# Shifts of transposed heads by pairs, and the reads of the second half's hash bits ahead of the normalized rows' transposing transfer

## The chip, the cores and the metric

The kernel runs on one core of one Trainium2 chip. The time is the device time of one execution in microseconds (us); of the kernel before, three runs are shown. Engines: PE is TensorE (matrix products), DVE VectorE, ACT ScalarE, POOL GpSimd, and SP is SyncE, which here only issues transfers (DMAs). Each engine works through its own queue in order; SP's queue too: an issue that waits for something holds up all issues behind it.

## The reference, cut to what matters

Attention in which a query sees only the keys of the same hash bucket (six signs of a projection make the bucket), and behind it a normalization and a two-layer perceptron with a residual, over 4 batches of 8 heads, 768 rows and 64 elements per head.

```python
q_bits = (einsum('bhsd,dk->bhsk', q, proj) > 0)        # 6 bits; k_bits likewise
mask = q_bucket[:, :, :, None] == k_bucket[:, :, None, :]
scores = where(mask, q @ k.T / sqrt(D), -1e9)
attn = softmax(scores) @ v                             # x: heads side by side, 512 wide
xn = (x - mean(x)) / sqrt(var(x) + 1e-6) * g_ln
out = x + relu(xn @ w_ch1) @ w_ch2                     # 512 -> 2048 -> 512
```

## The kernel before, in words

The rows of a batch are worked on in chunks of 256 query rows, three to a batch, twelve in all. Stage n runs the attention of chunk n on TensorE and ScalarE: twelve units, three to a pair of heads, each with scores (L530), exponentials (L540), products with the values (L565) and, at a pair's end, the division (L585 to L592). The scores of the next unit are emitted ahead of the products of the present one. Heads come in pairs 0 and 1, 2 and 3, 4 and 5, 6 and 7; the first two pairs are the first half, the others the second.

The mask is made by the scores' product itself. The operand tile `slots` (two of them, batches taking turns) holds for each head 64 rows of transposed data and under them, in rows 64 to 69, the six bits as plus or minus a large number: a product over 70 rows then gives the score plus a term that sinks all keys of other buckets.

For batches 1 to 3 these operands are prepared during earlier stages, a half (four heads) at a time, by steps with one letter each, followed by the batch and the half (J11: batch 1, second half):

- L loads queries and keys, W the values (SP; for batch 1 GpSimd's queue).
- N (`narrow`, L357) casts them to bf16 on GpSimd.
- T (`operands`, L380) issues four transposing transfers on SP, one per head. The queries and keys of a head become six blocks of 128 columns in 128 rows: rows 0 to 63 hold one chunk of rows of the sequence, rows 64 to 127 the next one.
- P (`shifted`, L388) is one transfer on SP that copies rows 64 to 127 of the four heads to rows 0 to 63 of the other six blocks of the same heads: 384 KB.
- B (`blocks`, L362) transposes 32 by 32 blocks on VectorE, H (`hashes`, L397 to L414) multiplies them with the projection on TensorE, turns the products into bits on VectorE and writes them to a tile in DRAM, `bits_d`, by SP.
- J (`bit_rows`, L420) issues four transfers on SP, one per head, that read `bits_d` into rows 64 to 69 of all twelve blocks of the head, 18 KB each. As P reads rows 64 to 127 of six of these blocks, J's transfer for a head has to come behind P's for this head.
- V (and Y, Z) casts and sums the values on GpSimd; Q sums squares on ScalarE.

The order within a stage is written out by hand in a dictionary of strings, `steps` (L927 on). Beside the letters above, `n` stands for the normalization of the chunk before (`norm`, L630 on): statistics and centring on VectorE, then on SP one transposing transfer of the normalized rows, `xnT<-xn` (L641), which waits for VectorE. `u` is one of eight up-projections (L674) with its rectification, the first of which needs `xnT`; `d` is one of eight parts of a down-projection (L715), after each fourth of which SP issues an output store (L724). The function `interleave` spreads this list evenly over the units, so that the engines' queues hold the steps in the order of the string. SP gets T, P, J, H's write, L, W, n's transfer and d's stores in that order.

In stage 2 the second half of batch 1 is prepared up to its shift (T11, H11, P11), and its reads of bits, J11, are the second word of stage 3, behind `n`. The scores that first need them are those of heads 4 and 5 in stage 3.

Of the kernel before, what the change touches and what calls it, by code (L numbers as in the profile page):

```python
# [30 lines left out]
def kernel(  # L31
# [11 lines left out]
    nc = tc.nc  # L43
    P = 128

    B, H, S, D = q.shape
# [146 lines left out]
    class Prep:  # L193
# [191 lines left out]
        def shifted(self, half):  # L385

            dst = self.pair_places(half)
            nc.sync.dma_start(out=dst[0:D, :, 1], in_=dst[D:P, :, 0])  # L388

        def hashes(self, half):  # L390

# [455 lines left out]
    def first_two():  # L847
# [77 lines left out]


    steps = {  # L927
# [284 lines left out]
```

## Time and profile before

| What | us |
|---|---|
| Median of 3 runs | 307.48 |
| Lowest and highest run | 304.97 and 308.14 |
| The profiled execution | 306.8 |
| Its span, first to last instruction | 305.0 |
| TensorE busy in it | 294.8 |
| ScalarE busy | 216.8 |
| VectorE busy | 179.8 |
| GpSimd busy | 91.0 |

The lines of the profile that follow give for an instruction its start in us from the span's start, its duration in us, its engine (SPq is SP's queue, PEld TensorE's weight load), its line in the kernel, its operation and `out<-in` by the names of the tiles; `x4` counts instructions that were merged into one line, and brackets hold the idle time of the engine before it and what ended it. A transfer's line on SPq covers its issue, not its landing. In the chain of work (lines without a line's tile sizes) a piece marked DMA runs from the issue to the landing. In the lists of waits stand the waiting operation, what it waited for, us in total, the number of times, and the longest. The lines of a source line's instructions give the shortest, the median and the longest duration in ns and the first and last start in us.

### The profile page before, as it was taken

Reading aid. Unit: us, or ns where it says so; the run is one execution under the profiler, and the core shown is the slowest. Engines: PE = TensorE matmul, PEld = TensorE weight load, DVE = VectorE, ACT = ScalarE, POOL = GpSimd, SP = SyncE. Lnnn points to the kernel's source line nnn. Section 1 sums busy time; section 2 is a strip of 40 time slices with the busy share of each in tenths; the row PEclk is TensorE's granted clock in tenths of the full one; section 3 lists DMA queues with packets and bytes.
Section 4 is the critical chain, followed back from the end, with each engine's and each line's share of the span. In section 5 each row is a group of like instructions: output and inputs, shape, how many; then the busy total and the mean of one; then the engine's idle time right before and its main releaser. Section 6 shows DMA issues by size and latency. Waiting matters only on the chain.

```text
span 305.0 us, 7962 instructions
## 1 busy us (share of the span) xinstructions
PE 294.8 (97%) x3279; PEld 224.6 (74%) x3306; DVE 179.8 (59%) x420; ACT 216.8 (71%) x271; POOL 91.0 (30%) x119
## 2 busy tenths in 40 slices
PE   8899999999899999999999999999999999999994
PEld 6577896687587688678688678679678678687573
DVE  2778568755287576645865874834734745645422
ACT  3898987767687787788698688778698568575020
POOL 2999721791011145160650740100100100100200
PEclk9999999999999999999999999999999999999998
DMA  7999999949589767695397365330220200200302
GB/s 214 359 220 252 250 242 242 191 82 151 98 261 204 155 212 128 176 289 138 97 234 192 109 111 124 41 89 2 21 84 2 69 37 2 71 35 2 105 2 74
DMA packets 58617, 40.93 MB, mean 134 GB/s; under 512 B 38576, under 2 KB 53424, under 8 KB 58576
## 3 DMA queue, kind: packets, MB, share of 16 engines
q1 hardware_dynamic: 53712, 30.80, 44.4%
q0 software_dynamic: 4288, 8.91, 12.5%
q10 hardware_dynamic: 576, 0.66, 0.7%
q8 instruction: 27, 0.44, 0.6%
q14 instruction: 14, 0.11, 0.1%
HBM read 27.98 MB, written 6.88 MB: 114 GB/s over the span
## 4 chain that ended last, share of the span: by engine, by line
PE 76%; DMA 7%; POOL 5%; ACT 4%; DVE 3%; issue 2%; SPq 2%; POOLq 0%; ACTq 0%; DVEq 0%
PE hp L674 25%; PE o L715 19%; PE sc L530 17%; PE av L565 9%; ACT ex L540 3%; DMA qnat<-in_q_dram 2%; PE hash L397 2%; DMA slots<-slots 1%; SPq L380 1%; POOL vsum L440 1%; PE o L697 1%; DMA xnT<-xn 1%; PE tpose L231 1%; POOL vaug L431 1%; POOL nat L357 1%
## 5 line engine op out<-in xcount | busy, mean ns | idle before, releaser
L540 ACT ACTIVATE ex<-sc,expb 128x1024 bf16<-128x1024 f32 x144 | 159.4, 1112 | 55.3 <-PE sc L530 53.8
L674 PE MATMUL hp<-xnT,w_sb 128*128 128x256 bf16 x768 | 98.3, 272 | 0.5 <-ACT hbuf L686 0.2
L715 PE MATMUL o<-w_sb,hbuf 128*128 128x512 bf16 x341 | 89.8, 379 | 1.2
L530 PE MATMUL sc<-slots 70*128 70x256 bf16 x576 | 86.5, 272 | 3.1 <-DMA slots<-bits_d 1.2
L674 PEld LDWEIGHTS <-w_sb 128*128 128x128 bf16 x768 | 71.7, 98 | 9.5 <-DMA xnT<-xn 0.8
L530 PEld LDWEIGHTS <-slots 70*128 70x128 bf16 x576 | 51.8, 97 | 17.8 <-issue 1.7
L565 PEld LDWEIGHTS <-ex 128*128 128x128 bf16 x1152 | 54.0, 98 | 14.4 <-issue 1.2
L684 DVE TENSOR_SCALAR hbuf<-hp 128x512 bf16<-128x512 f32 x49 | 33.7, 687 | 44.3 <-PE hp L674 44.2
L565 PE MATMUL av<-vaug,ex 128*128 128x65 bf16 x1152 | 58.6, 194 | 0.2 <-ACT ex L540 0.2
L628 POOL TENSOR_SCALAR rs<-mv 128x2 f32<-128x2 f32 x12 | 8.6, 717 | 150.8 <-DVE mv L612 150.7
L715 PEld LDWEIGHTS <-hbuf 128*128 128x128 bf16 x368 | 33.5, 97 | 25.4
L686 ACT ACTIVATE hbuf<-hp 128x512 bf16<-128x512 f32 x47 | 27.9, 593 | 17.2 <-PE hp L674 17.2
L720 DVE SCALAR_TENSOR_TENSOR x<-o,rs,x 128x512 f32<-128x512 f32 x23 | 17.1, 742 | 23.4 <-PE o L715 23.3
L592 DVE TENSOR_TENSOR x<-av,rc 128x256 f32<-128x256 f32 x48 | 20.4, 424 | 1.6
L585 DVE TENSOR_SCALAR rc<-av 128x4 f32<-128x4 f32 x36 | 5.6, 156 | 24.8 <-PE av L565 24.8
L617 DVE SCALAR_TENSOR_TENSOR xn<-x,mv,gbc 128x512 bf16<-128x512 f32 x24 | 17.8, 748 | 0.7
L611 DVE BATCH_NORM_STATS2 stats<-x 128x6 f32<-128x512 f32 x24 | 16.5, 687 | 0.4
L586 DVE TENSOR_TENSOR av<-av,vsum 128x256 f32<-128x256 f32 x36 | 15.6, 432 | 1.2
L357 POOL CAST nat<-qnat 128x1536 bf16<-128x1536 f32 x6 | 8.8, 1464 | 24.1 <-DMA qnat<-in_q_dram 14.6
L431 POOL CAST vaug<-vnat 128x1536 bf16<-128x1536 f32 x8 | 11.8, 1472 | 7.4 <-DMA vnat<-in_v_dram 7.3
L211 ACT ACTIVATE knat<-knat 128x768 f32<-128x768 f32 x16 | 13.4, 836 | 0.0
L211 ACT ACTIVATE qnat<-qnat 128x768 f32<-128x768 f32 x16 | 13.3, 833 | 0.0
(87 smaller groups left out, 205.5 us busy)
## 6 DMA issues: line engine op xcount, KB each, us to landing
out_dram<-x SPq DMA_DIRECT2D x23, 256.0 KB
vnat<-in_v_dram SPq DMA_DIRECT2D x6, 768.0 KB
w_sb<-in_moe_w_ch_dram POOLq DMA_DIRECT2D x4, 1024.0 KB, 13.6
knat<-in_k_dram SPq DMA_DIRECT2D x10, 384.0 KB
qnat<-in_q_dram SPq DMA_DIRECT2D x8, 384.0 KB
slots<-slots SPq DMA_DIRECT2D x6, 384.0 KB
qnat<-in_q_dram POOLq DMA_DIRECT2D x2, 768.0 KB, 12.6
knat<-in_k_dram POOLq DMA_DIRECT2D x2, 768.0 KB, 13.9
```

What stands on the lines that cost most here:

```text
L211: nc.scalar.activation(src, src, AF.Square, accum_out=sq[:, a, col : col + 1],)
L530: nc.tensor.matmul(sc[:, i, :], key_block(h, kj), query_blocks(h),)
L540: nc.scalar.activation(ex, sc, AF.Exp, bias=expb[:, 1:2] if b else expb[:, 0:1], scale=scale if b else scale / Q_SCALE,)
L565: nc.tensor.matmul(av[:, h - ha, qi, :], state[g][:, i, qi * P : (qi + 1) * P], va[:, h, kj, :], start=(b > 0 and (g, i, qi) == (0, 0, 0)) ...
L592: nc.vector.tensor_tensor(xv, num, rc.unsqueeze(3).to_broadcast([P, 2, TT, D]), op=AOP.mult)
L611: nc.vector.bn_stats(stats, x[:, i, :])
L617: nc.vector.scalar_tensor_tensor(xn[:, :, i, :], x[:, i, :].rearrange("p (o d) -> p o d", d=P), mv[:, i, 0:1], gbc.rearrange("p (o d) -> p ...
L674: nc.tensor.matmul(hp[:, i, :], w1_sb[:, dt, nt * P : (nt + 1) * P], st["xnT"][:, dt, :], start=(dt == 0), stop=(dt == ND - 1),)
L684: nc.vector.tensor_scalar_max(dst, src, 0.0)
L686: nc.scalar.activation(dst, src, AF.Relu)
L715: nc.tensor.matmul(o2, st["h"][:, nt, i * P : (i + 1) * P], w2_sb[:, nt, :], start=(nt == 0), stop=(nt == NH - 1),)
L720: nc.vector.scalar_tensor_tensor(x[:, i, :], o2, st["rs"][:, i : i + 1], x[:, i, :], op0=AOP.mult, op1=AOP.add,)
```

## The change

The shift of a half is issued as two transfers, one for each pair of heads, instead of one for four heads. It holds for all six shifts (batches 1 to 3, two halves each). And J11, the reads of the second half's bits of batch 1, moves from stage 3, where it stood behind the norm, to stage 2, right behind P11; in SP's queue it so stands ahead of the transposing transfer of the normalized rows of stage 3. Nothing else is moved, and the bytes are the same.

```diff
         def shifted(self, half):
 
             dst = self.pair_places(half)
-            nc.sync.dma_start(out=dst[0:D, :, 1], in_=dst[D:P, :, 0])
+            for j in range(0, H // 2, 2):
+                nc.sync.dma_start(out=dst[0:D, j : j + 2, 1], in_=dst[D:P, j : j + 2, 0])
...
     steps = {
-        2: "n d d H10 P10 d d x Y10 W11 Z10 N11 J10 d N11 B11 d T11 B11 d B11 d B11 u H11 u P11 u u V11 u u u u",
-        3: "n J11 L20 d d d d W20 d d N20 d N20 d T20 u B20 u u B20 u u B20 P20 u B20 u u",
+        2: "n d d H10 P10 d d x Y10 W11 Z10 N11 J10 d N11 B11 d T11 B11 d B11 d B11 u H11 u P11 J11 u u V11 u u u u",
+        3: "n L20 d d d d W20 d d N20 d N20 d T20 u B20 u u B20 u u B20 P20 u B20 u u",
```

## The prediction

> **What bounds the kernel now.** I read the page first, then who waited for whom on TensorE between 30 and 282 us, then the chain and the order of time around the one long wait, on PE and on SP's queue.
>
> ```profile
> span 305.0 us, 7962 instructions
> PE 294.8 (97%) x3279; PEld 224.6 (74%) x3306; DVE 179.8 (59%) x420; ACT 216.8 (71%) x271; POOL 91.0 (30%) x119
> PE 76%; DMA 7%; POOL 5%; ACT 4%; DVE 3%; issue 2%; SPq 2%; POOLq 0%; ACTq 0%; DVEq 0%
> ```
> ```profile
> PE sc L530 <- DMA slots<-bits_d: 1.2, 1, 1.2
> PE sc L530 <- ACT ex L540: 0.4, 2, 0.3
> PE hp L674 <- ACT hbuf L686: 0.2, 1, 0.2
> ```
> ```profile
> 81.07 0.41 PE L565 MATMUL av<-vaug,ex 128*128 128x65 bf16 x8
> 82.69 0.61 PE L530 MATMUL sc<-slots 70*128 70x256 bf16 x4 [1.21 <-DMA slots<-bits_d]
> 84.36 0.82 PE L674 MATMUL hp<-xnT,w_sb 128*128 128x256 bf16 x6
> ```
>
> TensorE is the bound: busy 97% of the span. Between the opening and the tail only one wait of it is worth a term: 1.21 us at 81.48 (81.07 + 0.41), in stage 3, where the first scores of heads 4 and 5 of batch 1 wait for the bits of head 4. A microsecond won or lost there reaches the end, since no other engine takes over in that stretch: the two other rows of the list are 0.4 and 0.2 us. So the largest gain this change can have is about 1.2 us, 0.4%. What released the wait stands in the chain and in SP's queue:
>
> ```profile
> 72.80 2.83 DMA slots<-nat
> 75.72 4.24 DMA slots<-slots
> 79.97 2.68 DMA slots<-bits_d
> ```
> ```profile
> 54.47 0.53 SPq L414 DMA_DIRECT2D bits_d<-bits  x1
> 58.13 0.70 SPq L388 DMA_DIRECT2D slots<-slots  x1
> 58.92 0.54 SPq L724 DMA_DIRECT2D out_dram<-x  x1
> 64.26 3.17 SPq L420 DMA_DIRECT2D slots<-bits_d  x4
> 67.48 6.61 SPq L380 DMA_TRANSPOSE slots<-nat  x4
> 74.20 0.52 SPq L724 DMA_DIRECT2D out_dram<-x  x1
> 74.82 0.37 SPq L414 DMA_DIRECT2D bits_d<-bits  x1
> 75.72 0.68 SPq L388 DMA_DIRECT2D slots<-slots  x1
> 76.56 2.16 SPq L641 DMA_TRANSPOSE xnT<-xn  x1
> 79.97 3.04 SPq L420 DMA_DIRECT2D slots<-bits_d  x4
> 83.12 0.44 SPq L140 DMA_DIRECT2D qnat<-in_q_dram  x1
> ```
>
> The reader sees a queue that is a chain from end to end: transposes of the second half (67.48, last one landing at 72.80 + 2.83 = 75.63), its shift (75.72, landing 79.96), the reads of its bits (79.97, the first landing 82.65), TensorE at 82.69. The normalized rows' transposing transfer (76.56) takes 2.16 us of issue, until 78.72, but the reads start only at 79.97, when the shift lands: they wait for the shift, not for the transfer ahead of them. Moving the reads alone would therefore win nothing.
>
> Further up the same queue is a second wait of that kind:
>
> ```profile
> L388 SPq EVENT_SEMAPHORE  x12: 28/28/2966, 55.1 to 184.5; - x12
> ```
> ```profile
> L420 SPq EVENT_SEMAPHORE  x6: 17/17/4714, 59.5 to 199.1; - x6
> ```
> ```profile
> 60.72 1.46 POOL L357 CAST nat<-qnat 128x1536 bf16<-128x1536 f32 x1
> 62.13 1.47 POOL L357 CAST nat<-knat 128x1536 bf16<-128x1536 f32 x1
> ```
>
> SP begins to wait for the last of the first half's four transposes at 55.1 and issues the shift 2.97 us later; then it stands 4.71 us from 59.5 until that shift lands at 64.2. Behind this wait stand the first half's reads (64.26) and the second half's four transposes (67.48), whose operands GpSimd had finished at 63.6 (62.13 + 1.47). The transposes start the moment the reads are issued (64.26 + 3.17 = 67.43). The chain view names GpSimd before them, but the queue shows no gap there.
>
> **The change part by part.**
>
> (1) The first half's shift by pairs. The first pair needs only the transposes of two heads and is free to go at about 55.1, behind the bits' store (54.47 + 0.53), 3.0 us earlier than now; the second pair goes at 58.1 as the whole did, with half the bytes. The whole took 64.2 - 58.13 = 6.1 us here, against 4.24 for the same shift at 75.72. Charged with all 6.1 us, the first pair lands by 61.2, and the first two reads go while the second pair is under way. The second pair lands at 64.2 at the latest (nothing saved), at 62.4 if the time behind the 2.68 us of a small transfer halves with the bytes (58.13 + 2.68 + 1.7 = 62.5, rounded); I take 63.3, the middle. Two of four reads are left then, 1.6 us of the 3.17, so the second half's transposes start at 64.9 instead of 67.48: 2.6 us earlier. Bounds: 63.6 (GpSimd) and 65.8 (64.2 + 1.6). That the halves are told apart by head is an inference from the trace: TensorE took head 4 at 82.69, when the four reads had not even all been issued (79.97 + 3.04 = 83.01).
>
> (2) The second half's shift. The transposes take 8.16 us here from first issue to last landing (67.48 to 75.63) and less elsewhere:
>
> ```profile
> 93.02 5.93 SPq L380 DMA_TRANSPOSE slots<-nat  x4
> 100.52 0.68 SPq L388 DMA_DIRECT2D slots<-slots  x1
> 101.32 2.17 SPq L641 DMA_TRANSPOSE xnT<-xn  x1
> ```
>
> There it is 7.5 us (93.02 to 100.52, when the shift behind them is let go). From 64.9 they land at 72.4 to 73.1. The first pair goes behind their issue (5.93 to 6.61 us) and two stores (1.1 us as now, 74.09 to 75.19): 71.9 to 72.6, take 72.3. A half lands between 2.68 us (a transfer of 18 KB, the first read of bits) and 4.24 us (the whole) later; I take 3.4, the middle: 75.7. The second pair, let go at about 73, lands by 77.2 even if it takes the whole 4.24.
>
> (3) The reads of the second half, now before the norm. Four, 0.78 us apart as now (3.04 and 3.17 us for four): 75.7 to 78.8. The first lands 2.68 us after its issue, 78.4. TensorE asks at 81.48, so the wait of 1.21 us is gone with 3.1 us to spare: minus 1.21 us.
>
> (4) What the reads are moved past: the normalized rows' transposing transfer, now at 78.8 instead of 76.56, and behind it on SP the loads of batch 2 (83.12), an output store and the load of values. Who waits for the transfer is the first up-projection, 84.36 now and 83.15 with the wait gone. The transfer's cost to landing:
>
> ```profile
> 283.74 3.23 DMA xnT<-xn
> ```
> ```profile
> 70.10 2.65 SPq L380
> ```
>
> 3.23 us alone in the tail; the nearest row for a held one is the third transpose at 70.10, whose issue took 2.65 instead of about 1.28 us, 1.4 more, so 4.6. Landing between 82.0 and 83.4; I take 82.6, since the reads leave little data behind them. TensorE at 83.15 is met with 0.5 us in hand: cost 0, at most 0.3. If that cover is gone, every microsecond is paid in full. The loads of batch 2 go at about 80.1 (78.8 + 1.3) instead of 83.12, so the queue is ahead of itself from there on: no cost.
>
> (5) The other four shifts, stages 3 to 7, and six more issues in all. An issue costs SP 0.68 us for the whole shift; a half costs between 0.34 and 0.68. The first pair's falls into the wait for the last transposes, and the second's replaces the whole's. Nothing of it is on TensorE's path: the transfer behind the shift at 100.52 has until stage 4's up-projection. The one tight place is stage 5:
>
> ```profile
> 132.83 0.44 PEld L674 LDWEIGHTS <-w_sb 128*128 128x128 bf16 x5 [0.16 <-DMA xnT<-xn]
> ```
>
> Here the weights already wait 0.16 us for the transposed rows. With TensorE 1.2 us ahead they must come 1.2 us sooner. They should: the shift ahead of them goes half earlier, and the queue runs 3 us ahead since stage 3. Cost 0, at worst the 1.2 us again.
>
> The sum: -1.21 + 0 + 0 = -1.2 us, between -1.4 (the 0.16 us goes too) and -0.9. On the profiled execution, 306.8 us with a span of 305.0, that gives 305.6. Its 306.8 is 0.7 below the median of the runs, 307.48, which becomes 306.3 us.
>
> One rule speaks against splitting. The Trainium skill, DMA: Bandwidth & Descriptors, section "Measured (HBM→SBUF, 128 partitions, SWDGE, issued from GpSimd)", advises to batch transfers to 1 MiB or more, and its section "Anatomy of one DMA — SWDGE (gpsimd) path" gives each about 2.0 us that don't depend on size. By it, an estimate: two halves one behind the other would end 2.0 us later than the whole, at each of the two shifts, and the sum would be about +2.5 us instead of -1.2. The trace speaks against the serial reading: four transposes, each with a landing of about 2.8 us, end 8.16 us after the first's issue and not 11.3. It stays as the third rival, worked out from rows.
>
> **The rivals.**
>
> First, the one on the other side: the transposes don't start earlier, because the reads of bits wait for both halves of the shift or the second pair lands no sooner. Place: SP's queue in stage 3. From 67.48 the first pair of the second half goes at 75.2 and lands at 78.6, the reads take until 81.8, and the normalized rows land 3.23 to 4.6 us later, 85.0 to 86.4. TensorE would take the scores at 81.48 but stop at 83.15 for 1.9 to 3.3 us: the old wait of 1.21 is traded for a longer one, net +0.7 to +2.0 us, 308.2 to 309.5, middle 308.8. It decides from the point where the reads end later than 79.2 (83.15 - 3.9), so with transposes starting after about 65.3; between, gain turns into loss. For it speaks how near 64.9 lies to that point; against it, that the first pair is free 3 us earlier.
>
> Second, the gain is handed back in stage 5: the 0.16 us there says that the rows are just in time. If they come no sooner than now, TensorE waits there 1.2 us more: 307.5 us, no change. Against it speaks that everything ahead of it on SP moves up.
>
> Third, the halves run one behind the other, each with its 2.68 us. The first half's second pair then lands up to 2.7 us later (66.9), the transposes start at 68.5, the second half's reads end near 84.4 and the rows land at 88.3, against 84.36 now: +3.9 us, 311.4.
>
> **How the numbers follow.** Forecast 0.67, first rival 0.20, second 0.08, third 0.05. The likeliest gives 306.3 us. Its own range is 304.0 to 307.0: the lowest run shown, 304.97, less 1.0, and the median less 0.5. The whole range goes to 308.9 for the first rival's middle; its upper half and the third are left out. One per cent, 3.1 us, is about what a measurement of this kernel can tell from no change (the runs before lie 304.97 to 308.14). Faster by more than that: 0.05, since no term exceeds 1.4 us and only the spread of runs could show it. Slower: 0.09, the third rival and the upper end of the first. Within: 0.86.
>
> **What would show it.** Right: on SP the second half's first transposes near 64.9, its first pair of the shift near 72.3, reads near 75.7, the transposing transfer near 78.8; no wait of TensorE on bits near 81.5; an up-projection at about 83.2. Two reads at 59.6 to 61.2 show that pairs are told apart. Wrong in step 1: all four reads of the first half after 64. Wrong in step 4: a wait of the up-projection for the normalized rows in stage 3. Wrong in step 5: the wait of 0.16 us in stage 5 grown to over 1. A gain of over 2 us, or a new wait on another engine, would show that I read the bound wrongly.

## The result, and the profile after

The changed kernel takes 304.03 us (median of 18 runs, 303.57 to 308.96), the kernel before 307.77 us (18 runs, 304.97 to 310.73). The ratio is 0.9898, with a 95% interval of 0.9875 to 0.9921: about 1.0%, or 3.1 us; the difference of the medians is 3.7 us. Disturbed runs are left out of the ratios here and below. The forecast was 306.3 us, a gain of 1.2 us. Two and a half times as much came. That 304.03 still lies at the lower edge of the likeliest case's range, 304.0 to 307.0, is luck: this edge was the lowest run shown less 1.0, and no term of the sum reaches it.

The profiled execution took 304.0 us, with a span of 302.1. First the span, the engines' busy time and the chain's shares of its page:

```profile
span 302.1 us, 7969 instructions
PE 293.6 (97%) x3279; PEld 224.4 (74%) x3306; DVE 179.4 (59%) x420; ACT 216.7 (72%) x271; POOL 91.0 (30%) x119
PE 91%; ACT 3%; DVE 2%; issue 1%; DMA 1%; POOL 1%; ACTq 0%; SPq 0%
```

The chain that ended last is TensorE's for 91% instead of 76%. The detour over transfers and GpSimd (7% and 5% before) has all but left it. SP's queue in order of time (all line numbers from 388 on are one higher than before):

```profile
54.80 0.69 SPq L415 DMA_DIRECT2D bits_d<-bits  x1
56.12 2.03 SPq L389 DMA_DIRECT2D slots<-slots  x2
58.23 0.55 SPq L725 DMA_DIRECT2D out_dram<-x  x1
58.98 5.03 SPq L421 DMA_DIRECT2D slots<-bits_d  x4
64.91 6.16 SPq L380 DMA_TRANSPOSE slots<-nat  x4
71.18 0.52 SPq L725 DMA_DIRECT2D out_dram<-x  x1
71.81 0.37 SPq L415 DMA_DIRECT2D bits_d<-bits  x1
72.28 1.42 SPq L389 DMA_DIRECT2D slots<-slots  x2
75.07 3.08 SPq L421 DMA_DIRECT2D slots<-bits_d  x4
78.33 1.29 SPq L642 DMA_TRANSPOSE xnT<-xn  x1
79.66 0.57 SPq L140 DMA_DIRECT2D qnat<-in_q_dram  x1
```

This is the forecast queue within 0.7 us: transposes at 64.91 (64.9 forecast), the second half's first pair at 72.28 (72.3), its reads at 75.07 (75.7), the normalized rows at 78.33 (78.8), the loads of batch 2 at 79.66 (80.1). The first of these agrees by luck. The reads of the first half end at 64.01 (58.98 + 5.03), and the transposes then stand 0.9 us more until GpSimd has cast their operands, at 64.88:

```profile
63.42 1.46 POOL L357 CAST nat<-knat 128x1536 bf16<-128x1536 f32 x1
```

In the forecast the reads ended last, at 64.9, and GpSimd's 63.6 was only a bound. Next, who waited on TensorE between 30 and 282 us, and TensorE around the place of the old wait:

```profile
PE sc L531 <- ACT ex L541: 0.4, 2, 0.3
```
```profile
80.20 0.41 PE L566 MATMUL av<-vaug,ex 128*128 128x65 bf16 x8
80.45 0.60 PE L531 MATMUL sc<-slots 70*128 70x256 bf16 x4
80.89 1.03 PE L716 MATMUL o<-w_sb,hbuf 128*128 128x512 bf16 x4
82.11 1.04 PE L675 MATMUL hp<-xnT,w_sb 128*128 128x256 bf16 x8
```

The scores at 80.45 follow the products at once; no bracket stands behind them, where 1.21 us stood before. The up-projection at 82.11 has none either, so the rows, sent later, were in time. Of the three waits of the list before only the one for the exponentials is left. Up to here the queue and the wait went as forecast, and the sum should have been 1.2 us. It was not, so the experiments ask where the rest came from.

The best ruler for that is the start of the exponentials, of which there are 144, twelve to a stage. These rows of ScalarE before and after are the first exponential of stage 2, and before's first of stage 4:

```profile
45.58 1.11 ACT L540 ACTIVATE ex<-sc,expb 128x1024 bf16<-128x1024 f32 x1 [0.32 <-PE sc L530]
95.03 1.11 ACT L540 ACTIVATE ex<-sc,expb 128x1024 bf16<-128x1024 f32 x1 [0.85 <-PE sc L530]
```
```profile
44.72 1.11 ACT L541 ACTIVATE ex<-sc,expb 128x1024 bf16<-128x1024 f32 x1 [0.33 <-PE sc L531]
```

The changed kernel reached stage 2 already 0.86 us earlier (45.58 - 44.72), ahead of the first instruction that the change touches, which issues behind 54 us. Stages 2 and 3 took before 49.45 us (95.03 - 45.58). The same subtraction was made for every profile; the table below has the results.

### The profile page after: what moved, and what is told of

It is laid out like the page before. It is cut to its first block, busy times and chain, and to the rows that moved or that the text cites. A ratio compares the mean times of both kernels' runs of the same rounds, so it can differ in the third digit from the quotient of the medians.

```text
span 302.1 us, 7969 instructions
## 1 busy us (share of the span) xinstructions
PE 293.6 (97%) x3279; PEld 224.4 (74%) x3306; DVE 179.4 (59%) x420; ACT 216.7 (72%) x271; POOL 91.0 (30%) x119
## 4 chain that ended last, share of the span: by engine, by line
PE 91%; ACT 3%; DVE 2%; issue 1%; DMA 1%; POOL 1%; ACTq 0%; SPq 0%
PE hp L675 28%; PE o L716 23%; PE sc L531 20%; PE av L566 11%; PE hash L398 3%; ACT ex L541 3%; PE tpose L231 1%; PE o L698 1%; DMA xnT<-xn 1%; PE wakep L861 1%; POOL slots L269 1%; PE hash L312 1%; PE sums L456 0%; DVE xn L618 0%; DVE stats L612 0%
## 5 line engine op out<-in xcount | busy, mean ns | idle before, releaser
L687 ACT ACTIVATE hbuf<-hp 128x512 bf16<-128x512 f32 x47 | 27.9, 593 | 17.1 <-PE hp L675 17.1
```

Of the source, the lines that this page charges most:

```text
L687: nc.scalar.activation(dst, src, AF.Relu)
```

## The experiments

**First set of runs: the parts of the change.** The letters are the theories' names in the expectations. Theory A is the forecast's: the gain is the vanished wait, and what is above 1.2 us is that wait being longer in other executions. Its main rival D: the wait also lowers TensorE's granted clock behind it and so costs more than its length. Four kernels tell the parts apart: the pairs without the move, the move without the pairs, only the first half of batch 1 by pairs, and the kernel before once more with a profile.

split_only, the pairs at all six shifts, with J11 left in stage 3:

```diff
-            nc.sync.dma_start(out=dst[0:D, :, 1], in_=dst[D:P, :, 0])
+            for j in range(0, H // 2, 2):
+                nc.sync.dma_start(out=dst[0:D, j : j + 2, 1], in_=dst[D:P, j : j + 2, 0])
```

> All six shifts by pairs, the second half's reads of bits still behind the norm. Theory A (the first half's shift by pairs lets the whole queue of SP run ahead, and with it the wait for bits in stage 3 goes): ratio to before 0.988 to 0.993, about that of the whole change (0.990); the second half's transposes start near 65, no wait of TensorE on bits over 0.3 us. Theory B (the reads had to be moved as well, since they still wait behind the transposing transfer): ratio 0.995 to 1.000, and a wait on bits of 0.5 us or more stays.

It took 305.57 us against 307.54, ratio 0.9948 (0.9910 to 0.9985). SP's queue:

```profile
64.42 5.25 SPq L380 DMA_TRANSPOSE slots<-nat  x4
...
72.11 1.42 SPq L389 DMA_DIRECT2D slots<-slots  x2
76.06 1.29 SPq L642 DMA_TRANSPOSE xnT<-xn  x1
77.44 3.10 SPq L421 DMA_DIRECT2D slots<-bits_d  x4
```

The pairs alone bring the transposes to 64.42, and the reads, still behind the normalized rows, go at 77.44. The wait for bits is gone without the move, which for this wait only adds reserve: 75.07 instead of 77.44. The ratio lies between what the two theories expected.

move_only, the whole shifts, with J11 behind P11:

```diff
-        2: "... u H11 u P11 u u V11 u u u u",
-        3: "n J11 L20 d d d d ...",
+        2: "... u H11 u P11 J11 u u V11 u u u u",
+        3: "n L20 d d d d ...",
```

> The reads of the second half's bits ahead of the norm, all shifts whole. Theory A: no gain, since the reads wait for the shift and not for the transfer that stood ahead of them; the rows of the norm come late instead: a wait of the first up-projection of stage 3 of 1.5 to 3.5 us, ratio 1.000 to 1.010, transposes of the second half start near 67.5. Theory B: ratio 0.995 or below, and no such wait.

309.04 us, ratio 0.9987 (0.9939 to 1.0035): no gain. The median of all twelve executions is 1.5 us above the kernel before's (307.54), and single ones reach 313.64. SP, TensorE, and two stretches of 4 us (their length, the busy time of PE, PEld, DVE, ACT and POOL, then the granted clock, the share of the DMA engines and GB/s):

```profile
78.06 3.02 SPq L420 DMA_DIRECT2D slots<-bits_d  x4
81.20 1.29 SPq L641 DMA_TRANSPOSE xnT<-xn  x1
```
```profile
85.97 1.86 PE L674 MATMUL hp<-xnT,w_sb 128*128 128x256 bf16 x8 [3.22 <-DMA xnT<-xn]
```
```profile
84.00:88.00 4.00, 2.03 (x10) 1.43 (x10) 0.60 (x4) 0.00 (x0) 0.00 (x0) 0.68 0.78 252
88.00:92.00 4.00, 4.00 (x27) 2.88 (x25) 1.52 (x2) 1.93 (x3) 1.90 (x2) 0.50 1.03 377
```

This is the first rival, made to happen: the reads wait for the whole shift, the rows behind them are late, and the up-projection waits 3.22 us. What the rival did not have: inside this wait, at 85.41, the clock falls to half for 6.83 us, which doubles the price. Stages 2 and 3 take 54.09 us in this profile, 6.4 us more than in the changed kernel (47.65). The Trainium skill, TensorE: Matmul & The Clock Gate, section "Why this matters for your kernels", asks for no idle gap above about 3 us on TensorE; the 3.22 us agree. Moving the reads alone wins nothing, as the forecast said; it needs the pairs.

split_first, pairs only for the first half of batch 1:

```diff
+            step = 2 if (self.b, half) == (1, 0) else H // 2
+            for j in range(0, H // 2, step):
+                nc.sync.dma_start(out=dst[0:D, j : j + step, 1], in_=dst[D:P, j : j + step, 0])
```

> Only the shift of the first half of batch 1 goes by pairs, all others whole, nothing moved. Theory A: nearly the whole gain, ratio 0.988 to 0.994; the second half's transposes start near 65, its whole shift near 73, its reads near 77.5, the first landing near 80, and TensorE's wait for bits is gone or below 0.3 us. Theory B (the second half's own shift by pairs matters, or those of batches 2 and 3): ratio 0.996 to 1.000.

306.26 us, ratio 0.9941 (0.9904 to 0.9978): as much as all six shifts by pairs. Its transposes start at 65.56, its reads at 77.56, and no wait for bits is left. One shift of six is enough to take that wait away.

before_again is the kernel before.

> The kernel before, unchanged, to see how its wait for bits varies from execution to execution. Theory A (the profile of before showed a mild case: its execution took 306.8 us, the median of 18 runs is 307.8): the wait for bits in stage 3 differs by a microsecond or more between executions, and in this one lies between 0.5 and 4 us; ratio 0.998 to 1.002. Rival C (the wait is always 1.2 us, and what is beyond it in the measured gain comes from somewhere else, such as the opening): wait 1.1 to 1.3 us again.

308.01 us, ratio 0.9986 (0.9945 to 1.0027), and in its profile no wait for bits at all. Its reads went at 80.67, later than in the first profile (79.97), but TensorE asked later too: its opening was slower (the first exponential of stage 2 starts at 48.72, against 45.58). TensorE's waits there, and the stretches of 3 us:

```profile
PE sc L530 <- POOL slots L269: 0.9, 1, 0.9
PE tpose L231 <- DMA knat<-in_k_dram: 0.8, 1, 0.8
PE tpose L231 <- DMA qnat<-in_q_dram: 0.3, 1, 0.3
```
```profile
9.00:12.00 3.00, 2.33 (x28) 1.16 (x27) 2.75 (x6) 2.24 (x3) 1.93 (x4) 1.00 1.07 365
12.00:15.00 3.00, 2.42 (x13) 1.85 (x14) 0.69 (x1) 1.35 (x3) 2.58 (x5) 0.74 1.08 365
15.00:18.00 3.00, 3.00 (x31) 2.15 (x29) 1.55 (x3) 1.97 (x3) 2.77 (x4) 0.69 0.89 205
```

TensorE waited 1.1 us in sum for the first loads, and the clock was then halved for 3.41 us, from 13.44 on. The wait for bits is a race between SP's chain and TensorE's way through the opening, and it can be 0 in the kernel before. Theory A's longer wait fell.

**Second set: is it the clock behind the wait?** Here before took 306.51 us. The first two kernels repeat the change and split_only.

> The changed kernel, unchanged, on the same chip as the next three. Theory D (the gain beyond the wait seen in one profile is the clock and the spread: the wait of the kernel before differs between executions, and where it is long TensorE's granted clock falls to half for 3.4 us or more, which doubles its price): ratio 0.988 to 0.992, clock under 0.996 in at most 2 of 12 executions.

305.02 us, ratio 0.9947 (0.9904 to 0.9991).

> All shifts by pairs, the reads behind the norm, beside the changed kernel on one chip. Theory D: the reads wait behind the transposing transfer, which waits for VectorE until 76, so the first bits have a margin of about 1 us instead of 3; in some executions the wait comes back. Ratio 0.992 to 0.996, between the change and the kernel before, more spread than the change, clock under 0.996 in 2 to 5 of 12. Rival E (moving the reads has no part in it once the shifts are by pairs): same median as the changed kernel within 0.3 us.

304.80 us, ratio 0.9968 (0.9929 to 1.0008). By the times the pairs alone are as good as the whole change here (rival E).

awake is the kernel before with ten products that nobody needs, 128 by 256, ahead of the scores that wait, so that TensorE stays busy in the wait:

```diff
+                    if (b, t, j, g) == (1, 0, 2, 0):
+                        for _ in range(10):
+                            nc.tensor.matmul(sc[:, 0, :], wake, w1_sb[:, 0, 0:CT])
```

> The kernel before with ten products of 256 columns (about 1.1 us) of constants in front of the scores that wait for bits in stage 3, written where these scores then write; they fill the wait and keep TensorE busy. Theory D (half the price of the wait is the clock that falls behind it): fewer executions under a clock of 0.996 than the kernel before, median lower by 0.3 to 1.5 us, although work was added. Rival F (the clock has no part in it): the clock falls as often, median the same or up to 1.1 us higher.

307.31 us, ratio 1.0013 (0.9966 to 1.0061): no gain from keeping TensorE busy is measured. The mean clock was below 0.996 in 5 of 12 executions, and in 13 of 35 of the kernel before beside it.

hold is the changed kernel with a wait added at the same place (a product whose weights VectorE has to copy first):

```diff
+                    if (b, t, j, g) == (1, 0, 2, 0):
+                        hold = work.tile([P, d_model], BF16, tag="hold", bufs=1, name="hold")
+                        nc.tensor.matmul(sc[:, 0, 0:P], wake, wake)
+                        nc.vector.tensor_copy(hold[:, 0:P], sc[:, 0, 0:P])
+                        nc.vector.tensor_copy(hold, gbc)
+                        nc.vector.tensor_copy(hold, gbc)
+                        nc.tensor.matmul(sc[:, 0, 0:P], hold[:, 0:P], wake)
```

> The changed kernel with a wait of TensorE made on purpose at the place of the old one: before the first scores of heads 4 and 5 in stage 3 a small product, a small copy of it by VectorE, two copies of 128 by 512, and a product that reads the last; TensorE stands 1.2 to 1.8 us, with no transfer in it. Theory D: slower than the changed kernel by the wait and, in a part of the executions, by 1.7 us or more beyond it, with a clock of 0.994 or less there: median +1.5 to +3.0 us. Rival F: +1.2 to +1.8 us in all executions, clock 1.0 as in the changed kernel.

```profile
82.40 0.23 PE L536 MATMUL sc<-wake,hold 128*128 128x128 bf16 x1 [1.31 <-DVE hold L535]
```

306.43 us, 1.4 more than after_again on the same chip: a wait of 1.31 us costs about its own length there, and in this profile the clock stays whole behind it, as it does behind the waits for bits of the kernel before (0.71 to 1.32 us in three profiles). So nothing speaks for theory D at these lengths. One point stays open: the mean clock was below 0.996 in 4 of 12 executions of hold and in 2 of 12 of the change beside it, and where it fell in those was not recorded.

**Third set, one profiled execution each: how much does the kernel before vary?** Theory G: the wait for bits is what a slow opening leaves of it, a fixed time on SP's side less TensorE's own. Three more profiles of the kernel before, and the second half of batch 1 alone by pairs.

> The kernel before once more, for a profile. Theory G (the wait is what is left of a race: the transfers' side of SP's queue takes the same time from the start of the program, TensorE's side depends on how long its opening took, so a slow opening hides the wait): with the ninth exponential at t, the wait for bits is about 23.7 - t, and none above that, within 0.7 us. Rival H (the wait varies with the transfers themselves, independent of the opening): no such relation, waits over 2 us among these profiles.

> As before_p1. Beside it: a fall of the granted clock shows where it happens. Theory G: in the opening, before 20 us, where short waits follow one another. Rival D (behind the wait in stage 3): between 80 and 90 us.

> The kernel before a third time, with the same two questions: the wait for bits against the time of the ninth exponential (theory G: 23.7 us less that time; rival H: unrelated), and where the granted clock falls, if it does.

TensorE at the scores in the first two, in this order; and for the third, which has no such wait, TensorE's waits in the opening and the stretch that follows them:

```profile
82.72 0.61 PE L530 MATMUL sc<-slots 70*128 70x256 bf16 x4 [0.71 <-DMA slots<-bits_d]
```
```profile
82.44 0.61 PE L530 MATMUL sc<-slots 70*128 70x256 bf16 x4 [1.32 <-DMA slots<-bits_d]
```
```profile
PE tpose L231 <- DMA qnat<-in_q_dram: 1.8, 2, 1.7
```
```profile
18.00:21.00 3.00, 3.00 (x28) 1.53 (x29) 1.41 (x4) 1.21 (x2) 2.79 (x4) 0.54 1.14 213
```

Wait 0.71, 1.32 and 0 us, times 307.02, 307.99 and 309.53. The slowest of the three is the one without the wait: its opening had the halved clock. So the wait is worth 0 to 1.3 us in the kernel before, 0.65 on average over five profiles (1.21, 0, 0.71, 1.32, 0), and a late opening hides it.

> Only the shift of the second half of batch 1 goes by pairs, nothing moved. Theory A: the second half's transposes start as before, near 67.5; its first pair goes about 0.5 us earlier than the whole did and lands about 1 us earlier, so the wait for bits shrinks by 1 to 2 us but the queue does not run ahead: reads near 78.5 instead of 80. Rival I (the pairs of this half matter as much as those of the first): no wait on bits and a queue as early as in the full change.

split_second has the diff of split_first with (1, 1) in the condition. Its one execution took 305.43 us, with transposes at 66.47, reads at 77.65 and no wait. It was then timed:

> Only the second half's shift of batch 1 by pairs, now timed. Theory J: the wait on bits is gone in most executions, the 0.4 us wait on rectification stays: ratio 0.993 to 0.998. Rival K: 0.990 or below, or 0.999 or above.

306.75 us, ratio 0.9989 (0.9956 to 1.0022), and its profile has a wait at the same place again. SP's queue and TensorE:

```profile
69.60 5.37 SPq L380 DMA_TRANSPOSE slots<-nat  x4
...
79.19 3.25 SPq L422 DMA_DIRECT2D slots<-bits_d  x4
```
```profile
82.62 0.60 PE L532 MATMUL sc<-slots 70*128 70x256 bf16 x4 [1.65 <-issue]
```

The profile names nothing that ended this wait ("issue"); that it is the one for bits is read from its place and from the reads, issued 3.4 us before. Without the pairs in the first half the transposes begin at 66.47 in one execution and at 69.60 in another (over all ten profiles with a whole first shift 65.9 to 70.7, on average 67.9); with them they begin at 64.4 to 67.5, on average 65.7. Nor are the pairs always told apart: in after_third and after_fourth all four reads of the first half go together, from 63.44 and 63.04 on. Pairs in the second half alone don't secure the reads. Theory G held for the five profiles of the kernel before but is too simple: SP's side varies as well.

**Fourth and fifth set: do the later batches' shifts count?** By step 5 of the forecast they don't, so pairs for batch 1 alone, with the move, equal the change. The rival K: they do.

```diff
+            step = 2 if self.b == 1 else H // 2
+            for j in range(0, H // 2, step):
+                nc.sync.dma_start(out=dst[0:D, j : j + step, 1], in_=dst[D:P, j : j + step, 0])
```

> The change for batch 1 alone: its two shifts by pairs and its reads moved; the four shifts of batches 2 and 3 whole. Theory J (all of the gain comes from batch 1: the wait on bits, 0.4 us of a wait on rectification, and nothing from later batches): the times of the whole change, ratio 0.988 to 0.996; stages from 95 us on as long as in the kernel before. Rival K (the later shifts add something): ratio 0.997 or above.

> The changed kernel on the same chip as the three before. Theory J: ratio 0.988 to 0.996, the same as the change for batch 1 alone within 0.3 us; clock under 0.996 in at most 3 of 12. If the clock falls as often as in the kernel before (5 of 12 or more), the rarer falls seen so far were chance.

305.97 us for batch 1 alone, ratio 1.0002 (0.9963 to 1.0042), and 304.78 for the change, 0.9928 (0.9899 to 0.9957).

> The change for batch 1 alone, a second time. Its stages from the ninth exponential on were as short as those of the whole change, its time was not (1.0002). Theory M (the opening and its clock differ by chance between executions, not between these kernels): clock under 0.996 in 0 to 3 of 12, ratio 0.989 to 0.997. Rival K (the later shifts have a part after all): ratio 0.998 or above again, clock under 0.996 in 4 or more of 12.

> The changed kernel beside it on the same chip. Theory M: ratio 0.989 to 0.997 and within 0.003 of the change for batch 1 alone; clock under 0.996 in 0 to 3 of 12. Rival K: 0.005 or more below it.

306.03 us, ratio 0.9964 (0.9921 to 1.0007), against 304.51, 0.9889 (0.9829 to 0.9949). By the times K holds: 0.74 and 0.75% between the two ratios, 1.2 and 1.5 us between the medians. But the first two intervals only just miss each other and the second two overlap, and part of it is the clock: its mean was below 0.996 in 8 of the 24 executions of batch 1 alone and in 2 of the 17 of the change. The table below shows what of it the profiles bear out.

pad, the kernel before with six small transfers more on SP, near 270 us and ahead of the last chunk's normalized rows, as many as the change adds, should tell whether their mere number matters:

```diff
+        for i in range(6):
+            pad = bounce.tile([P, 2], BF16, tag="pad", bufs=6, name="pad")
+            nc.sync.dma_start(out=pad, in_=wake[:, 2 * i : 2 * i + 2])
```

> The kernel before with six small stores of 512 bytes on SP in a gap of its queue near 272 us: as many issues as the changed kernel, all shifts whole. If the opening and its clock differ between the kernels because of the number of SP's issues (rival L), the clock is under 0.996 in 2 of 12 or fewer and the median is 0.5 to 1 us under the kernel before. If not (theory M: the difference in the opening is chance or something else): as the kernel before, ratio 0.997 to 1.003, clock under 0.996 in 3 to 6 of 12.

316.82 us, ratio 1.0375 (1.0313 to 1.0437). The tail was disturbed: TensorE waited 7.08 us until 294.4, and the clock was halved for 10.24 us from 289.4 on. For its question it is inconclusive.

**Where the time lies.** Worked out from the start times of the 25th, the 49th and the last of the 144 exponentials and the span of each profile, in us:

| Profile | ahead of stage 2 | stages 2 and 3 | stages 4 to 11 | behind the last |
|---|---|---|---|---|
| before | 45.6 | 49.45 | 181.9 | 28.1 |
| before_p1 | 46.1 | 48.94 | 181.8 | 28.2 |
| before_p2 | 45.2 | 49.86 | 182.8 | 28.4 |
| before_again | 48.7 | 48.07 | 182.2 | 27.8 |
| before_p3 | 49.5 | 48.06 | 182.3 | 27.8 |
| after | 44.7 | 47.65 | 181.8 | 27.9 |
| after_again | 46.2 | 47.66 | 181.8 | 27.4 |
| after_third | 45.9 | 48.08 | 181.8 | 27.3 |
| after_fourth | 46.1 | 47.78 | 181.8 | 27.3 |
| batch1_only | 45.7 | 47.66 | 181.8 | 28.1 |
| batch1_again | 48.1 | 47.65 | 181.8 | 28.1 |
| split_only | 45.5 | 48.06 | 181.8 | 27.3 |
| split_only_again | 45.3 | 48.07 | 181.8 | 27.6 |
| hold | 45.1 | 49.25 | 181.8 | 27.9 |
| mean of before (5) | 47.0 | 48.9 | 182.2 | 28.1 |
| mean of the change (4) | 45.7 | 47.8 | 181.8 | 27.5 |
| difference | 1.3 | 1.1 | 0.4 | 0.6 |

The differences add up to 3.4 us, the mean spans (306.2 and 302.9) differ by 3.3, near what the runs measured.

- Stages 2 and 3: 1.1 us. The wait for bits is 0.65 on average, 0.76 by this ruler (each of the three waits lengthens its step by 0.18 us more than itself). The rest is mostly another wait, the third row of the forecast's list: an up-projection near 93 us that waits for a rectification on ScalarE. It costs 0.41 us by the ruler in all five profiles of the kernel before, and it goes with the move of the reads: none of the eight profiles with the reads in stage 2 has it, move_only included, while split_only and all others with the reads in stage 3 have it, except awake. The instructions of TensorE, ScalarE, VectorE and GpSimd stand in the same order before and after; what differs is that this up-projection waits for VectorE's semaphore and no longer for ScalarE's. That can cost as much: in after_third, which has 48.08, VectorE was late there, behind a block transpose that had waited 1.54 us for a load. The rows are before's and after_third's:

```profile
93.20 1.03 PE L674 MATMUL hp<-xnT,w_sb 128*128 128x256 bf16 x8 [0.25 <-ACT hbuf L686]
```
```profile
92.14 1.03 PE L675 MATMUL hp<-xnT,w_sb 128*128 128x256 bf16 x8 [0.26 <-DVE hbuf L685]
```

- Stages 4 to 11: 0.4 us, from single waits in three of the five profiles of the kernel before. In before_p2 it is one of 0.84 us in stage 4 for VectorE. In the two others it is the wait of stage 5 for the transposed rows; this row of before_p3 shows it at 0.57 us on the weights, where the forecast's row had 0.16. The change has none in any of its four profiles.

```profile
135.78 0.77 PEld L674 LDWEIGHTS <-w_sb 128*128 128x128 bf16 x8 [0.57 <-DMA xnT<-xn]
```

- Behind the last exponential: 0.6 us. Kernels with all shifts by pairs have 27.3 to 27.9 there (seven profiles), the others 27.8 to 28.4, pad left out. That goes with theory K, but no instruction of the change is in that stretch. Of the 0.6 us, 0.14 lies ahead of TensorE's restart behind the last transposing transfer (10.13 and 9.99 us on average). The other 0.43 lies between VectorE's last addition, behind which the last output store goes, and the end of the span: 3.08 to 3.59 us in the kernel before, 2.72 to 3.30 in the change. Executions of one and the same kernel so differ there by as much as the two kernels do. In batch1_only and batch1_again the last transposing transfer goes 0.34 us later behind the last exponential than in the change (7.15 against 6.81); split_first, whose later shifts are also whole, has that too, before and split_second do not. What delays it was not found.
- Ahead of stage 2: 1.3 us, and all of it is the two profiles with a halved clock (48.7 and 49.5). Without them before has 45.6 against 45.7: no difference.

The last point is about how often. Of the timed executions, 50 of 127 of the kernel before had a mean granted clock below 0.996, 5 of 47 of the change, 5 of 24 of split_only, 8 of 24 of batch 1 alone, 4 of 12 of hold. In the profiles of before the fall lay between 13 and 22 us. Where the clock stayed above, the medians of the spans are 303.9, 304.9 and 304.6 us before and 303.1, 302.9 and 302.1 after, in the second, fourth and fifth set: a gain of 0.8, 2.0 and 2.5 us. The rest of the gain in the medians goes with rarer falls of the clock; that these lie in the opening is read from the profiles alone. Why they are rarer, when neither the instructions nor the transfers there are changed, stays open: batch 1 alone and hold, which share most of the change, have them about as often as before. Over its four timings the change gave ratios of 0.9898, 0.9947, 0.9928 and 0.9889; a gain of 1.2 us would be 0.9961, which only the second of their intervals holds.

## Why the prediction was wrong, point by point

Step 1 (transposes at 64.9) and step 2 (first pair at 72.3) were right within 0.1 us in the first profile. For step 1 this is half luck: there the reads end at 64.01 and GpSimd's cast lets the transposes go, and in the change's other three profiles they start at 65.18, 66.67 and 66.27. The reason holds on average: with the first half by pairs the transposes start 2.2 us earlier (65.7 against 67.9), and split_first has no wait for bits. Step 3 was right: the wait is gone, with more reserve than needed, since split_only has none either. Step 4 was right: the rows came in time, cost 0. That cover was real: move_only, without the queue's lead, pays for its loss, and more than the rival's 1.9 to 3.3 us because the clock falls too.

Step 5 was right in its sign for stages 4 to 11: the wait of stage 5 did not grow, it went. Its cost of 0 for the later shifts is not confirmed for the tail, where kernels with them end about 0.5 us sooner, and by the times they were worth 0.7%; but the tail varies by as much between executions of one kernel, and the cause is open. The same step and step 4 looked only at what the earlier queue and the move could cost.

The step that failed is the sum, "-1.21 + 0 + 0 = -1.2 us", with "between -1.4 [...] and -0.9", carried over to a median of runs. Three things were mis-sized. The term of 1.21 us is one execution's: over five it is 0.65, between 0 and 1.32, because it is what a race leaves. The wait of 0.2 us for a rectification, third in the forecast's own list, was left at 0 without a reason: it stands in stage 3 in all five profiles, costs 0.41 us by the exponentials, and goes with the move. And everything outside stage 3 was taken as equal in both kernels, at 0. Measured are -1.1 us in stages 2 and 3, close to the sum but made up otherwise (luck, not a confirmation), -0.4 in stages 4 to 11, -0.6 in the tail and -1.3 ahead of stage 2. The reason given against a larger gain, that "no term exceeds 1.4 us", looked only at the terms in one trace, and the kernel before has costs that come and go: waits of 0.3 to 0.9 us in stages 4 and 5, and a lower clock in 4 of 10 executions. The forecast's sign for a bound read wrongly, a gain of over 2 us, came; but TensorE is busy 97% of the span in both profiles, so the bound was right and the terms along it were not.

Of the rivals the first is a real mechanism, shown by move_only, but not of this change; from 64.91 the reads end at 78.15 (75.07 + 3.08), 1 us ahead of its deciding point of 79.2. It came near: in after_third and after_fourth the reads end at 79.42 and 80.06, past that point, but TensorE reached the up-projection later too (83.28 and 83.67 against 82.11), and only after_fourth loses 0.12 us there by the exponentials. The second, the gain handed back in stage 5, was wrong. The third, halves one behind the other, is refuted by the queue of the first profile: the reads start 2.8 us behind the first pair's issue (75.07 - 72.28), and the second pair landed at 76.02, 1.0 us behind the first, not 2.68.

## What to carry to other kernels

A wait at the end of a race between a DMA queue and an engine is read from several executions; one trace gives a sample of it, and a forecast against a median needs the mean. A queue in order is freed at its earliest wait: halving the first transfer that others stand behind moved the whole chain by 2.6 us in the first profiles and by 2.2 us on average, while moving the reads at its end, alone, moved another consumer into the wait. A reordering can also change which engine an instruction elsewhere waits for, so small waits in the list deserve a term of their own. What the change does not touch has still to be given a range as wide as it varies between executions.

## What the runs showed of the hardware

The granted clock falls to half in steps of one length: 3.41 us (before_again, before_p3, batch1_again), 6.83 us (move_only, awake), 10.24 us (pad). The Trainium skill, TensorE: Matmul & The Clock Gate, section "What's actually happening", gives a free-running window of 3413 ns, and the steps agree with it. The trigger was not only one long gap: in before_again TensorE was busy 2.24 of the 3.41 us ahead of the fall (10.03 to 13.44), its longest wait on one load under 1 us, while a single wait of 1.31 us in hold left the clock whole. The busy time alone does not tell them apart either: counted in steps of 3.41 us from the clock's rise at 6.13, hold's stretch with the wait (81.22 to 84.63) has TensorE busy for 2.23 us, as little as in the opening. What does was not tried.

Half a shift of 192 KB costs SP about as much issue as the whole of 384 KB (median 0.65 us against 0.68). Two halves overlap: issued 0.8 us apart (72.28 and 73.06), they landed 1.0 us apart (75.01 and 76.02).
